# Seven products instead of eight for seven pairs of weight chunks, summed in PSUM; the first w_out chunk cut by column halves; slack for single operations of the plan

## The chip, the core and the metric

The kernel runs on one core of a Trainium2 chip. The metric is the device time of the program in microseconds, the median of its runs; beside it stands one profiled execution with a trace of every instruction on TensorE (PE, its weight loads apart as PEld), VectorE (DVE), ScalarE (ACT), GpSimd (POOL) and SyncE (SP, which issues nearly all transfers here).

## What is computed

A memory attention (4 batches, 8 heads, 576 positions, head size 64, 32 memory slots) feeds two MLPs over 2304 tokens of width 512. In the reference's words, cut:

```python
a = softmax(phi)                                   # over the 32 slots
k_m, v_m = einsum("bhsm,bhsd->bhmd", a, k), einsum("bhsm,bhsd->bhmd", a, v)
x = softmax(q @ k_m^T / 8) @ v_m                   # 2304 x 512
h = x @ w_in;  g = maximum(0.01 * h, h)            # d_ff 2048
y = g @ w_out                                      # 2304 x 512
out = ((y @ w_a) * (y @ w_b)) @ w_out2             # d_ff 1536, all fp32
```

The weights are float64 in the reference and come to the kernel as 64-bit words, which it turns into fp32 itself. Most products run in three passes of the fast fp32r format (high x high, high x low, low x high); the first batch's tokens run in plain fp32 against the first chunks.

## The kernel before

**An order written out by a planner.** The code builds a list of operations (`op`), each with its engines and costs, the tiles it reads and writes, a place in the main sequence (`pos`) for the large products, and a `slack` that moves its due time. `Program.order` then walks through time with these costs and writes one fixed queue per engine; `SLACK`, `LEAD`, `START`, `BIAS`, `LAT`, `OVER`, `SPARE` steer it. Each engine runs its queue strictly in order, so what stands first in a queue holds up what stands behind it. SBUF is 29 "slot" tiles and some larger ones, PSUM 8 banks in rooms: "h" (3 banks), "y" (2), "x" (3); in the second MLP "ab" uses the six banks of "h" and "x", and the output products "o" and "os" share the two banks of "y".

**The start.** For batch b and head group g (0 or 1): phi is loaded, its maximum taken (DVE, `nmx`) and exponentiated (ACT), transposed on PE (`ta`, `tz`) into `en`; `km` multiplies it with the keys and values (tiles `kv`, two per group, and `kvr` for the last 64 positions of both groups), `kvn` normalises, `kvt` transposes, and the result goes into `kd` (keys) and `vm` (values). `vw` multiplies `vm` with a chunk of w_in; `sc` are the scores of one piece of queries (x = 0 or 1; for batch 0 piece 0 has 320 columns, piece 1 has 256), DVE makes the softmax of them through the tile `sm` (transpose, maximum, subtract, exponent on ACT, sum, multiply) and transposes them back to `at`. The first MLP's `h` product needs `at` and `vwf`. A piece of batch 0 and its four column blocks (f) is `h_n_f`; ACT applies the leaky rule into `gf`. `y` then multiplies with w_out: in chunk 0 the four tiles `wout_0` to `wout_3` are 128 rows of w_out by 512 columns, and every `y` needs all four. After loading, a weight tile takes two ACT and four DVE operations (`cv_...`) before PE may read it. `warm` runs 38 transposes of the identity on PE at the start, `idle` puts four more after certain early tiles.

**The second MLP** runs in two halves of the tokens (s = 0, 1), each over 12 chunks c of 128 columns of w_a and w_b. In `ab_unit` the two products y w_a and y w_b over two blocks of 512 tokens are seven block products of 512 columns each, by a Strassen-Winograd scheme: a bank X takes four of them one after the other, and ACT copies X out (`t1`, `u6`, `u67`) between two of them. Chunks are then taken in pairs for the output product with w_out2. For a pair there are two forms. **o_unit**: 8 units (2 token blocks, 4 output blocks) of 6 matmuls of 512 columns. **o_part** (where `by_seven` holds): `w2_sums` and `p_sums` make sums of the weights and of the products, and 14 units of 3 matmuls of 512 columns follow, each in its own PSUM group; the sums of each of the seven products over the pairs are kept in seven SBUF tiles, and combined once, after the last pair (`plus`). In the kernel before, `by_seven` holds for the second half's chunks 0 to 7, four pairs. In the first half a third, narrow block of tokens (l = 2, 256 columns) goes through `left_unit` and `o_unit`. The weights of the first `PRE` = 4 chunks of the second MLP are prepared during the first MLP. At the end SP writes the output, each 128x512 unit of the last block in two transfers of 320 and 192 columns.

## Time and profile before

| | |
|---|---|
| median of 3 runs | 787.19 us (787.18 to 787.81) |
| the profiled execution, its own time | 786.36 us |
| its span in the trace | 784.6 us |
| PE busy | 773.4 us (99%) |
| DVE busy | 607.2 us (77%) |
| ACT busy | 379.1 us (48%) |
| granted clock | 1.00 |

1.76 us of the profiled execution lie outside its span, and the median stands 0.83 us above the profiled execution. A busy time of a stretch is the share in which the engine had at least one instruction in work; matmuls overlap, so what one costs is read from start to start. "idle before" in brackets is how long the engine waited before a row, and for what.

### The profile page before, as it was taken

What the parts mean: (1) busy time and instruction counts of PE and PEld (TensorE: products, weight loads), DVE (VectorE), ACT (ScalarE), POOL (GpSimd) and SP (SyncE); (2) the same over time, 40 slices, a digit from 0 to 9 for tenths busy, and PEclk for the clock granted to TensorE, in tenths of its full rate; (3) what the DMA queues carried; (4) which work ended last, traced back from release to release, by engine and by line L of the source; (5) the groups of instructions that cost most, each with busy time, mean ns of one, the idle gap of its engine ahead of it and who ended that gap; (6) DMA issues with size and microseconds to landing.
All of it is one profiled execution on the core that took longest, in us unless ns stands there. A gap on an engine that the chain in (4) does not pass through costs nothing.

```text
span 784.6 us, 12658 instructions
## 1 busy us (share of the span) xinstructions
PE 773.4 (99%) x4822; PEld 663.4 (85%) x4822; DVE 607.2 (77%) x1149; ACT 379.1 (48%) x817; POOL 0.7 (0%) x6
## 2 busy tenths in 40 slices
PE   7899999999999999999999999999999999999997
PEld 6567898989898988998888888888888888888886
DVE  5888988868888865686745899998995667898865
ACT  5767777747465635453445454445332254223210
POOL 0000000000000000000000000000000000000000
PEclk9999999999999999999999999999999999999999
DMA  9993331573247300035867547475488586978503
GB/s 321 384 323 140 99 90 61 192 264 103 82 174 266 124 1 1 1 115 206 293 247 267 185 160 273 161 239 190 164 322 346 178 275 209 354 250 280 179 19 108
DMA packets 56557, 149.99 MB, mean 191 GB/s; under 512 B 7216, under 2 KB 22576, under 8 KB 56496
## 3 DMA queue, kind: packets, MB, share of 16 engines
q1 hardware_dynamic: 56496, 149.18, 54.5%
q8 instruction: 38, 0.62, 0.3%
q14 instruction: 23, 0.19, 0.1%
HBM read 103.55 MB, written 45.61 MB: 190 GB/s over the span
## 4 chain that ended last, share of the span: by engine, by line
PE 95%; DMA 2%; DVE 1%; SPq 0%; ACT 0%; issue 0%
PE y L871 24%; PE abx L1092 17%; PE o L1186 13%; PE h L821 13%; PE abz L1092 8%; PE os L1301 5%; PE aby L1092 4%; PE b L1146 2%; PE a L1146 2%; PE y L867 2%; PE vw L750 2%; DMA kv<-in_kv_dram 1%; DMA phi<-in_phiT_dram 1%; PE h L803 1%; PE km L603 1%; PE sc L667 0%
## 5 line engine op out<-in xcount | busy, mean ns | idle before, releaser
L871 PE MATMUL y<-g,wout 128*128 128x320 f32 (+2 forms) x1104 | 197.2, 333 | 0.0
L871 PEld LDWEIGHTS y<-g,wout 128*128 128x128 f32 x1104 | 175.6, 188 | 16.7 <-issue 2.1
L1092 PE MATMUL abx<-yb_T,wo 128*128 128x512 f32 x432 | 109.7, 389 | 0.0
L1103 ACT COPY t<-abx 128x512 f32<-128x512 f32 x72 | 42.3, 587 | 122.7 <-PE abx L1092 117.6
L1092 PEld LDWEIGHTS abx<-yb_T,wo 128*128 128x128 f32 x432 | 80.6, 188 | 16.4
L1186 PE MATMUL o<-p,wout 128*128 128x512 f32 x384 | 93.6, 389 | 0.0
L1186 PEld LDWEIGHTS o<-p,wout 128*128 128x128 f32 x384 | 71.9, 188 | 15.2 <-DVE osum L1199 0.4
L774 ACT ACTIVATE g<-h 128x256 fp32r<-128x256 f32 (+1 forms) x120 | 49.7, 414 | 52.9 <-PE h L821 50.8
L821 PE MATMUL h<-ahi,vwh 128*128 128x256 f32 (+1 forms) x240 | 72.7, 303 | 0.0
L821 PE MATMUL h<-ahi,vwl 128*128 128x256 f32 (+1 forms) x240 | 71.0, 296 | 0.0
L821 PE MATMUL h<-alo,vwh 128*128 128x256 f32 (+1 forms) x240 | 71.0, 296 | 0.0
L890 DVE TENSOR_TENSOR acc<-y,acc 128x320 f32<-128x320 f32 (+1 forms) x72 | 40.1, 557 | 36.6 <-PE y L871 35.7
L837 DVE TENSOR_TENSOR g<-t,g 128x256 fp32r<-128x256 f32 (+1 forms) x120 | 53.7, 453 | 15.4 <-ACT t L774 14.4
L821 PEld LDWEIGHTS h<-ahi,vwh 128*128 128x128 f32 x240 | 45.4, 189 | 10.2 <-issue 3.6
L774 ACT ACTIVATE t<-h 128x256 f32<-128x256 f32 (+1 forms) x120 | 49.5, 413 | 0.0
L821 PEld LDWEIGHTS h<-alo,vwh 128*128 128x128 f32 x240 | 45.4, 189 | 0.2
L821 PEld LDWEIGHTS h<-ahi,vwl 128*128 128x128 f32 x240 | 45.5, 190 | 0.0
L1100 DVE TENSOR_TENSOR t<-abz,t 128x512 f32<-128x512 f32 x48 | 33.0, 688 | 13.2 <-PE abz L1092 7.6
L1199 DVE TENSOR_TENSOR oacc<-o,oacc 128x512 f32<-128x512 f32 x40 | 27.6, 690 | 16.7 <-PE o L1186 16.2
L1092 PE MATMUL abx<-yb_B,wo 128*128 128x512 f32 x144 | 36.9, 391 | 0.0
L1092 PE MATMUL aby<-yb_B,wo 128*128 128x512 f32 x144 | 36.7, 390 | 0.0
L407 ACT CAST p<-t 128x512 fp32r<-128x512 f32 x32 | 19.9, 621 | 34.7 <-DVE t L1124 22.7
(289 smaller groups left out, 1276.1 us busy)
## 6 DMA issues: line engine op xcount, KB each, us to landing
k_wo<-wo SPq DMA_DIRECT2D x32, 512.0 KB, 4.4
wo<-k_wo SPq DMA_DIRECT2D x32, 512.0 KB, 4.9
raw_wout<-in_w_out_dram SPq DMA_DIRECT2D x24, 512.0 KB, 5.5
raw_win<-in_w_in_dram SPq DMA_DIRECT2D x16, 512.0 KB, 5.2
...
```

What stands on the lines that cost most here:

```text
L774: nc.scalar.activation(dst, src, AF.Prelu, alpha=0.01)
L821: nc.tensor.matmul(T[o], T[w[u]][:, k, fs], T[a[v]][:, k, cols], start=(k == 0 and i == 0), stop=(k == 1 and i == 2))
L837: lambda T, e: engines[e].tensor_tensor(T[g][:, i, 1, to], T[t], T[g][:, i, 0, to].bitcast(F32), op=ALU.subtract),
L871: nc.tensor.matmul(T[o], w[:, u, es], T[g][:, j, v, at:at + m], start=(f == 0 and p == 0), stop=(f == 3 and p == 2))
L890: "DVE", c_dve(m), lambda T: nc.vector.tensor_tensor(T[acc][:, i, :], T[o], T[acc][:, i, :], op=ALU.add),
L1092: nc.tensor.matmul(T[o], T[w][:, which, u, k * P:(k + 1) * P], T[ys[v]][:, k, :], start=first and k == 0 and x == 0, stop=k == 1 and x == ...
L1100: op("DVE", 0.69, lambda T: nc.vector.tensor_tensor(T[to], T[o], T[x], op=ALU.add), r=[o, x], w=[to], tiles=[o, x, to])
L1103: op("ACT", 0.59, lambda T: nc.scalar.copy(T[t], T[X]), r=[X], w=[t], tiles=[X, t])
L1146: nc.tensor.matmul(T[o], T[w][:, k // 2, u, k % 2 * P:(k % 2 + 1) * P], T[ys[v]][:, k, :], start=(k == 0 and x == 0), stop=(k == 3 and x = ...
L1186: nc.tensor.matmul(T[o], T[w][:, u, es], T[g][:, at, v, :], start=(x == 0 and k == 0), stop=(x == 1 and k == 2))
L1199: "DVE", c_dve(size), lambda T: nc.vector.tensor_tensor(T[acc][:, i, :], T[o], T[acc][:, i, :], op=ALU.add),
L1301: nc.tensor.matmul(T[o], lhs(T, u), T[g][:, v, :], start=k == 0, stop=k == 2)
```

## The change

1. **Seven products for seven pairs.** `SEVENS` lists the chunks for each half: 8 to 11 in the first, 0 to 9 in the second, so two pairs and five pairs.
2. **Summed in PSUM.** The 14 units of a pair stand in another order, and several share a bank: products 1, 6, 7 and 4 are added up in one bank, ACT copies the bank out after 1, 6 and 7 (tile `ok`), and DVE adds what is in the bank to one of four sums in SBUF; products 5 and 3 share another bank, product 2 has its own. There is no combination after the last pair; instead each pair adds the copies to the sums.
3. **w_out's first chunk by column halves.** Its four tiles now hold 256 output columns by 256 rows each, so that `y` for output blocks 0 and 1 reads tiles 0 and 1 only.
4. **The start.** The 256-column piece of batch 0 goes first (`FIRST`); batch 0's `km` is three operations that can start with the transfers that are there; copies into `kd` and `vm` are two operations; 22 transposes in `warm` instead of 38, and `idle` only after two tiles of w_in and after batch 0's `en`.
5. **The plan.** New constants, and `NUDGE`, a table that adds a slack to single operations by their number.
6. **The rest.** `PRE` = 5. The last unit of the output product is two units of 320 and 192 columns.

Counted in the queues: PE has 384 matmuls of 512 columns in `o` before and 234 after (and 6 of 320 and 6 of 192), 168 in `os` before and 294 after; all other products are as many as before; fills are 38 + 48 transposes before and 22 + 16 after. DVE has 1144 rows before and 1201 after, ACT 795 and 838, SP 307 and 321.

```diff
-PRE = 4
+PRE = 5
...
-WARM = 38
-SEVEN = 8
-LEAD = 37
...
+FIRST = (1, 0, *range(2, NPIECE))
+KM_FIRST = (((4,), (0, 1), (2, 3)), ((4,), (0, 1), (2, 3)))
+WARM = 22
+SEVENS = ((8, 9, 10, 11), tuple(range(10)))
+LEAD = 57
...
-        o.slack, o.soon = slack, soon
+        o.slack, o.soon = slack + NUDGE.get(o.seq, 0.0), soon
...
-        "wout": lambda c, k: w_out[c * FC + k * P:c * FC + (k + 1) * P, :],
+        "wout": lambda c, k: w_out[c * FC + k * P:c * FC + (k + 1) * P, :] if c else
+        w_out[2 * (k % 2) * P:2 * (k % 2 + 1) * P, k // 2 * 256:(k // 2 + 1) * 256].rearrange("(j p) f -> p j f", p=P),
...
-        if kind == "win" and c == 0:
+        if kind == "win" and c == 0 and k > 1:
...
-        if b < 2:
+        if b == 0:
             idle(en, lambda t: t[:, 0, :], (en, 0))
...
-                if b == 0:
-                    idle(fk, lambda t, i=i: t[:, i, x * n:x * n + P], (fk, i, x))
...
-        ws = [("wout", c, f) for f in range(4)]
+        ws = [("wout", c, f) for f in range(4)] if c else [("wout", 0, 2 * (e // 2) + i) for i in range(2)]
...
     def by_seven(s, c):
-        return s == 1 and c < SEVEN
+        return c in SEVENS[s]
...
-    O_PARTS = ((1, "A11", "B11"), (6, "S2", "T2"), (7, "S3", "T3"), (5, "S1", "T1"), (2, "A12", "B21"), (4, "A22", "T4"), (3, "S4", "B22"))
+    O_PARTS = ((1, "A11", "B11"), (2, "A12", "B21"), (6, "S2", "T2"), (7, "S3", "T3"), (4, "A22", "T4"), (5, "S1", "T1"), (3, "S4", "B22"))
...
+        bank = {2: "y", 5: "z", 3: "z"}.get(i, "x")
+        o, g = ("os", s, q, x, bank), ("pb", s, q, right)
+        if i in (1, 2, 5):
+            tile_of(o, "y", [NB2])
...
-                nc.tensor.matmul(T[o], lhs(T, u), T[g][:, v, :], start=k == 0, stop=k == 2)
+                nc.tensor.matmul(T[o], lhs(T, u), T[g][:, v, :], start=i in (1, 2, 5) and k == 0, stop=k == 2, skip_group_check=True)
...
+        if i in (1, 6, 7):
+            k = kept_of(i)
+            if x == 0:
+                tile_of(k, "slot", [2, NB2])
+            op("ACT", 0.59, lambda T: nc.scalar.copy(T[k][:, x, :], T[o]), r=[o], w=[(k, x)], tiles=[o, k])
+            return
+        d, m = {2: (2, 1), 4: (4, None), 5: (7, 7), 3: (3, 6)}[i]
...
-            for i in range({NC2 - 2: 4, NC2 - 1: 1}.get(c, 7) if s else 6):
+            for i in range({NC2 - 2: 6, NC2 - 1: 6}.get(c, 8) if s else 7):
...
+                        last = s == 1 and c == NC2 - 1 and l == 1 and e == 3
+                        for cols in [p[:2] for p in places_of(s, l)] if last else [None]:
+                            queue.append(lambda pos, s=s, c=c, l=l, e=e, cols=cols: o_unit(s, c - 1, l, e, pos, cols))
```

**In the queues, at the start.** SP's queue from the phi of batch 1 on, before (`raw_wout` are the tiles of w_out's first chunk; the q behind them are batch 1's queries):

```order
L557 DMA phi_293<-in_phiT_dram 128x1152
L567 DMA kv_0_0_297<-in_kv_dram 128x1024
L567 DMA kv_0_1_306<-in_kv_dram 128x1024
L567 DMA kv_1_0_331<-in_kv_dram 128x1024
L567 DMA kv_1_1_358<-in_kv_dram 128x1024
L570 DMA kvr_385<-in_kv_rest_dram 64x1024
L464 DMA raw_wout_0_397<-in_w_out_dram 128x512
L464 DMA raw_wout_1_414<-in_w_out_dram 128x512
L464 DMA raw_wout_2_427<-in_w_out_dram 128x512
L464 DMA raw_wout_3_475<-in_w_out_dram 128x512
L645 DMA q_0_493<-in_qT_dram 128x1152
```

The same stretch of SP's queue after:

```order
L562 DMA phi_225<-in_phiT_dram 128x1152
L572 DMA kv_0_0_246<-in_kv_dram 128x1024
L575 DMA kvr_265<-in_kv_rest_dram 64x1024
L572 DMA kv_1_1_272<-in_kv_dram 128x1024
L572 DMA kv_0_1_283<-in_kv_dram 128x1024
L572 DMA kv_1_0_300<-in_kv_dram 128x1024
L469 DMA raw_wout_0_315<-in_w_out_dram 128x2x256
L469 DMA raw_wout_1_341<-in_w_out_dram 128x2x256
L660 DMA q_1_349<-in_qT_dram 128x1152
L660 DMA q_0_373<-in_qT_dram 128x1152
```

The small `kvr` moved ahead of three `kv`, so that a `kv` of group 1 is the last of batch 1's inputs; two of the four w_out tiles moved behind the queries of batch 1.

DVE's queue up to the transpose that gives the first `at`, before (`sm_0` is the 320-column piece, `sm_1` the 256-column piece, each with both halves side by side; `er` is batch 1's):

```order
L542 TENSOR_SCALAR er_82<-es_81 128x2
L543 RECIPROCAL er_82<-er_82 128x2
L697 TENSOR_REDUCE mx_8_85<-sm_1_387 128x16
L698 TENSOR_TENSOR sm_1_387<-sm_1_387,mx_8_85 128x512
L702 TENSOR_REDUCE sr_10_84<-sm_0_361 128x20
L703 TENSOR_SCALAR sr_10_84<-sr_10_84 128x20
L704 RECIPROCAL sr_10_84<-sr_10_84 128x20
L707 TENSOR_TENSOR sm_0_361<-sm_0_361,sr_10_84 128x640
L702 TENSOR_REDUCE sr_8_86<-sm_1_387 128x16
L703 TENSOR_SCALAR sr_8_86<-sr_8_86 128x16
L704 RECIPROCAL sr_8_86<-sr_8_86 128x16
L711 STREAM_TRANSPOSE at_0_479<-sm_0_361 128x640
```

The same part of DVE's queue after:

```order
L547 TENSOR_SCALAR er_82<-es_81 128x2
L548 RECIPROCAL er_82<-er_82 128x2
L712 TENSOR_REDUCE mx_10_83<-sm_0_345 128x20
L717 TENSOR_REDUCE sr_8_86<-sm_1_313 128x16
L718 TENSOR_SCALAR sr_8_86<-sr_8_86 128x16
L719 RECIPROCAL sr_8_86<-sr_8_86 128x16
L713 TENSOR_TENSOR sm_0_345<-sm_0_345,mx_10_83 128x640
L722 TENSOR_TENSOR sm_1_313<-sm_1_313,sr_8_86 128x512
L626 TENSOR_SCALAR kvn_0_428<-km_0_380,er_82 128x256
L726 STREAM_TRANSPOSE at_1_430<-sm_1_313 128x512
```

Piece 1 comes first, the other piece's sum and its two companions stand behind the first `at`, and a `kvn` moved from ACT to DVE ahead of it. In both queues the reduction of batch 1's phi (`nmx`) stands earlier: before it precedes the transposes of piece 0's scores, after it stands behind those of piece 1's.

**In the queues, a pair of the second half.** PE's queue at the output product of chunks 8 and 9 before (`o_1_8_0_e`: second half, chunk 8, token block 0, output block e):

```order
L1186 MATMUL o_1_8_0_0_8021<-p_1_8_0_7854,wout2_8_1_7776 128x512 x3
L1186 MATMUL o_1_8_0_0_8021<-p_1_9_0_7989,wout2_9_1_7797 128x512 x3
L1186 MATMUL o_1_8_0_1_8034<-p_1_8_0_7854,wout2_8_1_7776 128x512 x3
L1186 MATMUL o_1_8_0_1_8034<-p_1_9_0_7989,wout2_9_1_7797 128x512 x3
L1092 MATMUL abx_1_10_7894<-yb_1_T4_0_1_6681,wo_1_10_1_7822 128x512
L1092 MATMUL abx_1_10_7894<-yb_1_T4_1_1_6697,wo_1_10_1_7822 128x512
L1092 MATMUL abx_1_10_7894<-yb_1_T4_0_1_6681,wo_1_10_1_7822 128x512 x2
L1092 MATMUL abx_1_10_7894<-yb_1_T4_1_1_6697,wo_1_10_1_7822 128x512
L1092 MATMUL abx_1_10_7894<-yb_1_T4_0_1_6681,wo_1_10_1_7822 128x512
```

PE's queue in the same pair's output product after (`os_1_4_1_x`: second half, pair 4, columns 1 of 2, the bank x):

```order
L1323 MATMUL os_1_4_1_x_8149<-pb_1_4_T2_8051,w2_1_4_0_7878 128x512 x3
L1107 MATMUL aby_1_11_8173<-yb_1_B21_0_1_6661,wo_1_11_0_7956 128x512
L1107 MATMUL aby_1_11_8173<-yb_1_B21_1_1_6672,wo_1_11_0_7956 128x512
L1107 MATMUL aby_1_11_8173<-yb_1_B21_0_1_6661,wo_1_11_0_7956 128x512 x2
L1107 MATMUL aby_1_11_8173<-yb_1_B21_1_1_6672,wo_1_11_0_7956 128x512
L1107 MATMUL aby_1_11_8173<-yb_1_B21_0_1_6661,wo_1_11_0_7956 128x512
L1323 MATMUL os_1_4_1_x_8149<-pb_1_4_T3_8060,w2_1_4_1_7953 128x512 x3
```

Where the pair was 8 units of 6 matmuls, each into a bank of its own, it is now 14 of 3, and here two of them go into one bank with one product of `ab` (6 matmuls) between them, in which time ACT copies the bank out.

**In the queues, the end.** PE's last rows before:

```order
L1186 MATMUL o_10_1_1_8208<-p_11_1_8161,wout_11_1_8028 128x512 x3
L1186 MATMUL o_10_1_2_8217<-p_10_1_8093,wout_10_1_8008 128x512 x3
L1186 MATMUL o_10_1_2_8217<-p_11_1_8161,wout_11_1_8028 128x512 x3
L1186 MATMUL o_10_1_3_8227<-p_10_1_8093,wout_10_1_8008 128x512 x3
L1186 MATMUL o_10_1_3_8227<-p_11_1_8161,wout_11_1_8028 128x512 x3
```

PE's last rows after:

```order
L1204 MATMUL o_10_1_2_8274<-p_11_1_8225,wout_11_1_8016 128x512 x3
L1204 MATMUL o_10_1_3_0_8284<-p_10_1_8138,wout_10_1_8006 128x320 x3
L1204 MATMUL o_10_1_3_0_8284<-p_11_1_8225,wout_11_1_8016 128x320 x3
L1204 MATMUL o_10_1_3_320_8294<-p_10_1_8138,wout_10_1_8006 128x192 x3
L1204 MATMUL o_10_1_3_320_8294<-p_11_1_8225,wout_11_1_8016 128x192 x3
```

The last unit became two, and the one that ends last has 192 columns.

## Rows read from the trace of the kernel before

**Rows 1.** The page: busy us, share, instructions; PE's busy tenths in 40 slices.

```profile
PE 773.4 (99%) x4822; PEld 663.4 (85%) x4822; DVE 607.2 (77%) x1149; ACT 379.1 (48%) x817; POOL 0.7 (0%) x6
...
PE   7899999999999999999999999999999999999997
```

**Rows 2.** Windows: length, busy us of PE, PEld, DVE, ACT, POOL; clock, DMA share, GB/s.

```profile
20.00:30.00 10.00, 9.21 (x131) 5.53 (x130) 7.35 (x15) 6.08 (x16) 0.00 (x0) 1.00 1.03 361
30.00:40.00 10.00, 8.43 (x75) 5.73 (x76) 9.87 (x22) 8.63 (x22) 0.00 (x0) 1.00 1.02 407
```

**Rows 3.** Timeline of PE: start, busy us, merged matmuls of one kind, count.

```profile
97.59 1.93 PE L871 MATMUL y<-g,wout 128*128 128x320 f32 x12
99.36 0.28 PE L821 MATMUL h<-ahi,vwh 128*128 128x256 f32 x1
...
586.67 1.60 PE L1146 MATMUL a<-yl,wo 128*128 128x256 f32 x12
...
595.04 2.88 PE L1186 MATMUL o<-p,wout 128*128 128x512 f32 x12
597.76 1.52 PE L1092 MATMUL abx<-yb_T,wo 128*128 128x512 f32 x6
```

**Rows 4.** Timeline of PE at the start; in brackets idle time before, and releaser.

```profile
19.98 2.35 PE L750 MATMUL vw<-cv_win,vm 64*32 64x256 f32 x32
22.26 1.09 PE L434 MATMUL warm<-ident,vwf 128*128 128x128 f32 x8
...
30.25 0.42 PE L603 MATMUL km<-kvr,en 64*32 64x128 f32 x8 [0.70 <-DMA kvr<-in_kv_rest_dram]
30.60 1.08 PE L603 MATMUL km<-kv,en 128*32 128x128 f32 x32
31.61 0.42 PE L603 MATMUL km<-kvr,en 64*32 64x128 f32 x8
...
33.01 3.50 PE L803 MATMUL h<-at,vwf 128*128 128x320 f32 x12 [0.33 <-DVE at L711]
...
39.46 2.86 PE L803 MATMUL h<-at,vwf 128*128 128x256 f32 x12 [0.78 <-ACT gf L774]
```

**Rows 5.** Timeline of DVE, from batch 1's phi to the first transposed scores.

```profile
22.92 1.35 DVE L531 TENSOR_REDUCE nmx<-phi 128x2 f32<-128x1152 f32 x1 [1.91 <-DMA phi<-in_phiT_dram]
24.31 0.91 DVE L688 STREAM_TRANSPOSE sm<-sc 128x320 f32<-128x320 f32 x2
...
28.97 0.81 DVE L702 TENSOR_REDUCE sr<-sm 128x20 f32<-128x640 f32 x1
29.82 0.17 DVE L703 TENSOR_SCALAR sr<-sr 128x20 f32<-128x20 f32 x1
30.03 0.28 DVE L704 RECIPROCAL sr<-sr 128x20 f32<-128x20 f32 x1
...
32.17 0.79 DVE L711 STREAM_TRANSPOSE at<-sm 128x640 f32<-128x640 f32 x1
```

**Rows 6.** Timeline at the end: DVE's last row, SP's last issues; a transfer's landing.

```profile
780.69 0.69 DVE L1199 TENSOR_TENSOR osum<-o,osum 128x512 f32<-128x512 f32 x1 [0.67 <-PE o L1186]
...
780.05 2.17 SPq L1205 DMA_DIRECT2D out_dram<-osum  x4
...
out_dram<-osum SPq DMA_DIRECT2D x4, 96.0 KB, 1.7
```

**Rows 7.** The tile `warm` from 1.3 to 5.8 us, then 6.3 to 7.9: ns min/median/max.

```profile
L426 PE MATMUL warm<-ident x21: 421/421/473, 1.4 to 5.7; 128*128 128x128 f32 x21
...
L426 PE MATMUL warm<-ident x16: 273/273/290, 6.1 to 7.8; 128*128 128x128 f32 x16
```

**Rows 8.** ACT's copies of the bank X: ns of one; idle us, times.

```profile
L1103 ACT COPY t<-abx x72: 578/587/590, 372.3 to 761.4; 128x512 f32<-128x512 f32 x72
...
  PE abx L1092: 117.6, 62
```

**Rows 9.** DVE alone in a window: length, busy us, clock, DMA share, GB/s.

```profile
431.96:528.24 96.28, 86.14 (x164) 1.00 0.59 202
```

More of the change, by code (lines that the diff above doesn't have):

```diff
@@ L531, in phi_stats @@
             "DVE", c_dve(S * len(gs)), lambda T: nc.vector.tensor_reduce(st[0][:, part], T[phi], axis=AX.X, op=ALU.max, negate=True),
-            r=e, w=nmx, tiles=[phi],
+            r=e, w=nmx, tiles=[phi], slack=SLACK["nmx"] if b else 0.0,
         )
@@ L596, in kv_part, with k_m @@
         tile_of(km, "x", [P])
-        def k_m(T):
-            for t in range(5):
+        def k_m(T, ts, first, last):
+            for t in ts:
                 n = P if t < 4 else 64
-                src = T[kvt[t // 2]][:, t % 2, :] if t < 4 else T[rest][:, g, :]
+                src = T[kvt[t // 2]][:, t % 2, :] if t < 4 else T[rest][:, g, 0:512]
                 for h in range(4):
@@ L604, in k_m @@
                         T[km][h * M:(h + 1) * M, :], T[en][0:n, t, h * M:(h + 1) * M], src[:, h * P:(h + 1) * P],
-                        start=(t == 0), stop=(t == 4),
+                        start=first and t == ts[0], stop=last and t == ts[-1], skip_group_check=True,
                     )
-        op("PE", 1.5, k_m, r=[(en, 0), (en, 1), *kvt, rest], w=[km], tiles=[en, *kvt, rest, km])
+        parts = KM_FIRST[g] if b == 0 else ((0, 1, 2, 3, 4),)
+        for i, ts in enumerate(parts):
+            need = list(dict.fromkeys(kvt[t // 2] if t < 4 else rest for t in ts))
+            op(
+                "PE", 0.29 * len(ts) + 0.05, lambda T, i=i, ts=ts: k_m(T, ts, i == 0, i == len(parts) - 1),
+                r=[(en, 0), *([(en, 1)] if 4 in ts else []), *need], w=[km], tiles=[en, *need, km],
+            )
         def norm(T, e):
@@ L670, in s_sc @@
                         )
-        op("PE", 4 * n / 2.4e3 + TURN, s_sc, r=[*qs, *(("kd", b % 2, g) for g in range(2))], w=scs, tiles=[*qs, *scs])
+        op("PE", 4 * n / 2.4e3 + TURN, s_sc, slack=SLACK["sct", x] if b == 0 else 0.0, r=[*qs, *(("kd", b % 2, g, i) for g in range(2) for i in range(2))], w=scs, tiles=[*qs, *scs])
         NM = n // 32
@@ L717, in sc_both @@
             lambda T, e: engines[e].tensor_tensor(T[alo][:, :, cols], T[at], T[ahi][:, :, cols].bitcast(F32), op=ALU.subtract),
-            r=[at, kh], w=[kl], tiles=[at, ahi, alo], slack=SLACK["sc", min(b, 2), x], ahead=1e12 if whole(0, b) else 60.0,
+            r=[(at, 0), (at, 1), kh], w=[kl], tiles=[at, ahi, alo], slack=SLACK["sc", min(b, 2), x], ahead=1e12 if whole(0, b) else 60.0,
         )
@@ L1314, in o_part @@
         tok = lambda i: (acc(i), x)
-        def plus(d, a):
-            op(
-                two(NB2), 0, lambda T, e: engines[e].tensor_tensor(part(T, d), part(T, d), part(T, a), op=ALU.add),
-                r=[tok(a)], w=[tok(d)], tiles=[acc(a), acc(d)], ahead=1e12, soon=True,
-            )
-        if q == 0:
-            op({"ACT": c_act(NB2), "DVE": c_dve(NB2)}, 0, lambda T, e: copy(e, part(T, i), T[o]), r=[o], w=[tok(i)], tiles=[o, acc(i)])
-            return
-        last = q == SEVEN // 2 - 1
@@ L1326, in o_part @@
-        op("DVE", 0.69, lambda T: nc.vector.tensor_tensor(part(T, i), T[o], part(T, i), op=ALU.add), r=[o], w=[tok(i)], tiles=[o, acc(i)])
-        if not last:
-            return
-        for d in {1: (2, 6), 6: (7, 3), 7: (4,), 5: (3, 7)}.get(i, ()):
-            plus(d, i)
+        kept_of = lambda j: ("ok", s, q, j)
+        if i in (1, 6, 7):
[4 more added lines that the diff above has]
+            return
@@ new lines, in o_part, with into @@
+        d, m = {2: (2, 1), 4: (4, None), 5: (7, 7), 3: (3, 6)}[i]
+        def into(T):
+            return T[acc(d)][:, x, :]
+        if q == 0 and m is None:
+            op({"ACT": c_act(NB2), "DVE": c_dve(NB2)}, 0, lambda T, e: copy(e, into(T), T[o]), r=[o], w=[tok(d)], tiles=[o, acc(d)])
+            return
+        k = kept_of(m) if m else None
+        if q == 0:
+            op("DVE", 0.69, lambda T: nc.vector.tensor_tensor(into(T), T[o], T[k][:, x, :], op=ALU.add), r=[o, (k, x)], w=[tok(d)], tiles=[o, k, acc(d)])
+            return
@@ new lines, in o_part @@
+        op("DVE", 0.69, lambda T: nc.vector.tensor_tensor(into(T), T[o], into(T), op=ALU.add), r=[o], w=[tok(d)], tiles=[o, acc(d)])
+        if m:
+            op(
+                two(NB2), 0, lambda T, e: engines[e].tensor_tensor(into(T), into(T), T[k][:, x, :], op=ALU.add),
+                r=[(k, x)], w=[tok(d)], tiles=[k, acc(d)], ahead=1e12, soon=True,
+            )
+        if 2 * q + 2 == NC2:
+            hh, l = PART[d]
+            for at, w_, to in places_of(s, l):
+                op(
+                    "DMA", c_dma(P * w_ * 4), lambda T, at=at, w_=w_, to=to: nc.sync.dma_start(out[:, 2 * hh + x, to:to + w_], T[acc(d)][:, x, at:at + w_]),
+                    r=[tok(d)], tiles=[acc(d)], ahead=1e12,
+                )
```

122 lines of the change are left out of this document (67 added, 55 removed).

## The prediction

> **What bounds the kernel now.** I read the page first: PE is busy 773.4 us of a span of 784.6, and its tenths are nines in all but the first, second and last of 40 slices [rows 1]. The reader should see that the loss is about 11 us and that nearly all of it lies before 40 us and after 780 us. Next the windows and PE's timeline at the start. From 30 to 40 us PE has 8.43 of 10 us, while DVE has 9.87 and ACT 8.63, the most loaded stretch of both [rows 2]. PE's waits there have three kinds of releaser: a transfer (`kvr`, 0.70 us), DVE (the first `at`, 0.33) and ACT (`gf`, 0.78) [rows 4]. Then the end: PE releases DVE's last addition at 780.69, and 3.9 us pass from there to the span's end at 784.6 with the addition, SP's last issues and a landing [rows 6]. Between 40 and 780 us work taken off PE is time gained one for one, as long as ACT and DVE keep pace; so I looked last at what ACT's copies and DVE have to spare there [rows 8, 9].
>
> The sum is made against the profiled execution, 786.36 us, of which 1.76 lie outside the span; the median of the runs is 0.83 above it. I take both as unchanged and apply the difference to the median, 787.19.
>
> **Seven products.** 512-column matmuls follow each other at (597.76 - 595.04)/12 = 0.227 us [rows 3]. A pair of chunks had 8 x 6 = 48 of them and now has 14 x 3 = 42. Three pairs more take the new form, so 18 go: 18 x 0.227 = **-4.1 us**. That is the difference of the counts too: 384 + 168 = 552 matmuls of 512 columns before, 234 + 294 = 528 after, where 6 of the 24 are the last unit, cut in two. No other work of PE changes after the start.
>
> **The last unit in two.** Six of 320 columns at (99.36 - 97.59)/12 = 0.147, and six of 192. The latter cost 0.085 by proportion to 0.227 and at most 1.60/12 = 0.133 by the row of 256 columns [rows 3]. That is 1.39 to 1.68 us for 6 x 0.227 = 1.36: 0.03 to 0.3, and I take **+0.1**, near the proportion.
>
> **The tail.** DVE's last addition falls from 512 to 192 columns. The two kinds of transposes, 0.79 us for 640 columns and 0.91/2 for 320 [rows 5], give about 1.05 ns a column, so 0.69 becomes 0.35: -0.34. Behind it stood two issues of SP and now one; four took 2.17 us [rows 6], 0.54 each, and as issues can overlap what precedes them I take -0.4 of 0 to -0.54. Together **-0.75** (-0.3 to -0.9). Against it: the last `o` units use the two banks of "y", and now additions of the last seven-product pair stand ahead on DVE. One bank can be late by up to one addition, 0.69 [rows 6], which PE then waits. I take **+0.5** (0 to 0.7), since the queue has such an addition directly ahead.
>
> **The first `h`.** Before, PE was held first by the last transfer of batch 1's inputs, `kvr` at 30.25, then ran `km` of group 1 to 32.03, and `h` began at 33.01 when DVE had `at` [rows 4]. After, as many bytes stand ahead of the last of these inputs, so it should land at 30.25 again, but it is `kv_1_0`. Only group 1's `km` follows, 32.03 - 30.60 = 1.43 us, and one `kvt`, two transposes at (7.8 - 6.1)/15 = 0.113 [rows 7], 0.23: `h` could begin at 30.25 + 1.43 + 0.23 = 31.9. For DVE both queues wait for the same phi, 22.92, and reduce it by 24.27 [rows 5]. Behind that the new queue lacks two transposes (0.91), the other piece's sum and its companions (0.81 + 0.17 + 0.28), and has two operations on 512 in place of 640 columns (about 0.3 less, by the slope above); it gains one `kvn`, about 0.4. `at` would be ready at 32.17 + 0.79 - 2.07 = 30.9, so PE and not DVE sets the start: **-1.1** (-2 if the transfer comes earlier, 0 if phi or `kv` come later, as SP's order past them is new). For this the first scores must be there by 21.1, 2.2 us before 23.29. Leaving out the fills of 22.26 (23.29 - 22.26 = 1.03) and starting the scores after half of `vw` (2.28/2 = 1.1) [rows 4] gives just that; what is late there comes out of DVE's margin of 1.0.
>
> ACT's wait at 39.46, 0.78 us [rows 4], comes as four w_out tiles and `gf` share ACT. With two of the four tiles behind batch 1's queries in SP's queue, half of that conversion leaves the stretch: **-0.6** (-0.8 to 0). The queries come two tiles earlier than that by the queue, so the scores that now stand between `h` products are covered, with about 0.8 us to spare.
>
> **What the new form asks of ACT and DVE.** ACT now has to copy a bank while PE runs one product of 6 matmuls, 6 x 0.227 = 1.36 us. The trace shows such copies at 587 ns, with ACT waiting for PE ahead of 62 of 72 [rows 8]: covered, unless the copy queues behind something of its own length. The queues have 36 such places; each can cost 0 or some tenths. DVE's load is the larger question. From the first addition of chunk 3 to that of chunk 8 of the first half it was busy 86.14 us in 96.28, in 164 instructions of 0.525 us on average [rows 9]. The new queue has 177 there: 93 us, in a stretch that gets no shorter than 95 (no seven-product pair ends in it, only the sums of its weights and `PRE`'s shift move). 98% against 89%. PE's slack there is the buffers' depth. I take **+1.0** for all of this: 0 by the covered copies, 6 if a sixth of a us is lost at each hand-off.
>
> The sum: -4.1 + 0.1 - 0.75 + 0.5 - 1.1 - 0.6 + 1.0 = -4.9, so **782.3 us** (the profiled execution 781.4, its span 779.7). With the bounds of the single terms, which won't fall on one side together, this case runs from 780.2 to 784.5; a start that gives nothing is inside it.
>
> **The rivals.** *The clock at the start.* Of the first 38 transposes the early ones last 0.421 us and those from 6.1 us on 0.273 [rows 7]: PE's pace rose after some 23 of them, back to back. The granted clock reads 1.00 in all windows [rows 2], the 2.4 GHz level, so the slow pace is seen in durations alone. With 22 the chain ends at about the point where the pace rose, and most of the fills behind it are gone. If PE keeps the slow pace until `h`, the `km`, `kvt` and `h` that now set the end are run at it: 0.7 us for the chain of 1.43 + 0.23 ahead of `h` (loads and waits in it don't double), and 2.4 for the first 4.75 us of dense work at half speed, the 4.75 being what the transposes took from 1.35 to 6.1. 782.3 + 3.1 = 785.4. For it: the row at 6.1. Against it: `ta`, `km`, `vw` and 16 fills still keep PE at work with gaps of under 1 us, except ahead of 30.25.
>
> The Trainium skill, "TensorE: Matmul & The Clock Gate", Part 4, says that PE's transposes do not count as busy for the clock gate. The trace disagrees, since the pace rose in a run of nothing but transposes [rows 7]. By the page the shorter `warm` would cost nothing and this rival would fall to the fills' share; by the rows it keeps its chance.
>
> *DVE becomes the bound of the first half* (the slower side). If DVE keeps idling a tenth of that stretch, as the row has it (10.1 of 96.28) [rows 9], because its work comes in the order of PE's banks, 93 + 10 = 103 us are needed where PE needs 95: PE waits 7.9 us for `ab` banks and sums where I put 1.0: 782.3 - 1.0 + 7.9 = 789.2. It decides from waits of about 7.5 us on. For it: 98%. Against it: an idle DVE was waiting for PE, and one that is behind does not idle.
>
> *Some of both*: hand-offs or DVE cost 3 to 5 us in place of 1: 784.3 to 786.3. *The start gives more* (both waits gone and the transfer earlier, no stall at the hand-offs): 779.3 to 780.5. That the change does not do what it says is excluded by the counts of the queues, 528 against 552.
>
> **How the numbers follow.** Forecast 0.58, clock 0.16, some of both 0.09, more 0.08, DVE the bound 0.09. About 0.2%, 1.6 us, is what a measurement can tell from no change: faster below 785.6, slower above 788.8. Faster: 0.58 + 0.08, 0.11 of the clock's 0.16 and 0.05 of the mixed case, 0.82. Within: 0.05 + 0.04 = 0.09. Slower: 0.09. The range leaves out DVE as the bound, a third of the "more" case and the mixed case's upper end, 0.15: 779.8 to 786.0.
>
> **What would show it.** Right: PE's gain between 40 and 780 us near 4; the first `h` near 31.9, with `kv_1_0` as the releaser ahead of it; no wait of 0.78 for `gf`; `os` rows waiting for ACT only by tenths; DVE over 95% in the first half with PE at 9s; a last addition of 0.35 with one issue behind. Wrong: the first 12 matmuls of `h` taking twice their 3.50 us for as many columns (the clock); rows of `ab` or `os` waiting for DVE by whole us between 430 and 530; `h` waiting for `at` (the scores came late); a bank wait over 0.7 before the last units.

## The result and the profile after

The kernel after takes **781.02 us** (median, 780.34 to 781.57) against 787.5 for the kernel before on the same chip: a ratio of 0.9914, interval 0.9897 to 0.9931. On another chip, beside three of the experiments, it took 781.68 against 787.4: 0.9926, interval 0.9913 to 0.9939. It is 5.7 to 6.5 us faster where 4.9 were forecast; 782.3 was predicted, 779.8 to 786.0 the range. The profiled execution took 781.57 with a span of 779.8, 4.8 us less than the span of before.

The page of after: busy us of each engine, PE's busy tenths, and the granted clock of PE in tenths.

```profile
PE 768.4 (99%) x4762; PEld 658.2 (84%) x4762; DVE 632.2 (81%) x1205; ACT 402.3 (52%) x856; POOL 0.7 (0%) x6
...
PE   7899999999999999999999999999999999999998
...
PEclk8999999999999999999999999999999999999999
```

PE is as full as before [rows 1], with 5.0 us less of work. New is the 8 at the front of the clock's row: before it was 9 throughout. The waits of PE from 40 us on, in the whole of after: us in total, times, the longest.

```profile
PE o L1204 <- DVE osum L1217: 0.5, 1, 0.5
```

So the place of the time is found by cutting the span at three starts of PE: the first `h`, the last `y` (at 375.4, 374.2 and 373.3 us in the three columns) and the last matmul of `o` (780.3, 776.5 and 776.3). "After, again" is the same kernel in a second profiled execution (label e12_after, span 779.6).

| stretch of PE | before | after | after, again | predicted change |
|---|---|---|---|---|
| start to first `h` | 33.01 | 32.85 (-0.2) | 31.90 (-1.1) | -1.1 |
| to the last `y` | 342.4 | 341.3 (-1.1) | 341.4 (-1.0) | -0.6 |
| to the last matmul of `o` | 404.8 | 402.3 (-2.5) | 403.1 (-1.8) | -4.1 + 0.1 + 0.5 + 1.0 = -2.5 |
| to the span's end | 4.3 | 3.3 (-1.0) | 3.3 (-1.1) | -0.75 |
| sum | 784.6 | 779.8 (-4.8) | 779.6 (-5.0) | -4.95 |

The same kernel begins `h` a microsecond apart in two executions, and gives the difference back in the second MLP. These two places are what most of the experiments are about. First the start, PE's timeline in after:

```profile
26.59 0.30 PE L592 MATMUL tz<-ident,phi 128*64 128x128 f32 x1 [1.74 <-ACT phi L542]
...
27.80 1.09 PE L589 MATMUL ta<-ident,phi 128*128 128x128 f32 x4 [0.43 <-DVE er L547]
...
29.03 1.90 PE L608 MATMUL km<-kv,en 128*32 128x128 f32 x32
...
31.21 1.08 PE L608 MATMUL km<-kv,en 128*32 128x128 f32 x32
...
32.85 1.46 PE L816 MATMUL h<-at,vwf 128*128 128x256 f32 x6
```

The `km` of group 0 takes 1.90 us where the same 32 matmuls of group 1 take 1.08, as they did in before [rows 4]. The granted clock tells why. Windows of after: length, busy us of PE, PEld, DVE, ACT, POOL; granted clock, DMA share, GB/s.

```profile
10.00:15.00 5.00, 3.87 (x40) 2.62 (x40) 3.19 (x8) 2.29 (x6) 0.00 (x0) 0.53 1.03 406
15.00:20.00 5.00, 4.39 (x61) 3.16 (x53) 2.89 (x7) 2.90 (x8) 0.00 (x0) 0.79 1.07 371
25.00:30.00 5.00, 2.98 (x30) 2.32 (x34) 4.90 (x12) 3.51 (x9) 0.00 (x0) 0.73 1.03 391
```

1.00 is the 2.4 GHz level and 0.5 the 1.2 GHz level; before, each of these windows reads 1.00. The clock fell at about 10 us, and again at 27 us, after PE had waited 1.74 us for the late phi. And phi was late: the reduction `nmx`, which waits for its landing, started at 24.28 where it had been 22.92 [rows 5]; in the second execution of the same kernel it was 23.25. DVE's timeline of after, then DVE's and PE's of after again:

```profile
24.28 1.35 DVE L536 TENSOR_REDUCE nmx<-phi 128x2 f32<-128x1152 f32 x1 [1.08 <-DMA phi<-in_phiT_dram]
```

```profile
23.25 1.35 DVE L536 TENSOR_REDUCE nmx<-phi 128x2 f32<-128x1152 f32 x1 [1.21 <-DMA phi<-in_phiT_dram]
...
27.99 1.89 PE L608 MATMUL km<-kv,en 128*32 128x128 f32 x32
...
30.26 1.08 PE L608 MATMUL km<-kv,en 128*32 128x128 f32 x32
```

### The profile page after: what moved, and what is told of

It reads as the page before. It is cut to its first block, busy times and chain, and to the rows that moved or that the text cites. A ratio compares the mean times of both kernels' runs of the same rounds, so it can differ in the third digit from the quotient of the medians.

```text
span 779.8 us, 12713 instructions
## 1 busy us (share of the span) xinstructions
PE 768.4 (99%) x4762; PEld 658.2 (84%) x4762; DVE 632.2 (81%) x1205; ACT 402.3 (52%) x856; POOL 0.7 (0%) x6
## 4 chain that ended last, share of the span: by engine, by line
PE 95%; DMA 3%; DVE 1%; SPq 0%; issue 0%
PE y L886 24%; PE abx L1107 17%; PE h L834 12%; PE o L1204 9%; PE abz L1107 8%; PE os_x L1323 5%; PE aby L1107 4%; PE os_z L1323 2%; PE b L1161 2%; PE a L1161 2%; PE y L882 2%; PE vw L765 2%; DMA phi<-in_phiT_dram 1%; PE os_y L1323 1%; DMA raw_win<-in_w_in_dram 1%; PE km L608 1%
## 5 line engine op out<-in xcount | busy, mean ns | idle before, releaser
L787 ACT ACTIVATE g<-h 128x320 fp32r<-128x320 f32 (+1 forms) x120 | 49.9, 416 | 68.1 <-PE h L834 63.8
L834 PE MATMUL h<-ahi,vwh 128*128 128x320 f32 (+1 forms) x240 | 72.1, 300 | 0.0
L834 PE MATMUL h<-ahi,vwl 128*128 128x320 f32 (+1 forms) x240 | 71.0, 296 | 0.0
L834 PE MATMUL h<-alo,vwh 128*128 128x320 f32 (+1 forms) x240 | 71.0, 296 | 0.0
L850 DVE TENSOR_TENSOR g<-t,g 128x320 fp32r<-128x320 f32 (+1 forms) x120 | 53.8, 454 | 10.3 <-ACT t L787 9.4
L1204 PE MATMUL o<-p,wout 128*128 128x512 f32 (+2 forms) x246 | 59.8, 385 | 0.5 <-DVE osum L1217 0.5
L1204 PEld LDWEIGHTS o<-p,wout 128*128 128x128 f32 x246 | 45.6, 188 | 10.3 <-DVE osum L1217 1.1
L787 ACT ACTIVATE t<-h 128x320 f32<-128x320 f32 (+1 forms) x120 | 49.9, 416 | 1.5 <-PE h L834 1.2
L1343 ACT COPY ok<-os_x 128x512 f32<-128x512 f32 x42 | 24.6, 587 | 25.6 <-PE os_x L1323 23.3
L1107 PE MATMUL abz<-yb_B,wo 128*128 128x512 f32 x144 | 36.6, 390 | 0.0
```

The lines of the kernel that those rows point to most:

```text
L787: nc.scalar.activation(dst, src, AF.Prelu, alpha=0.01)
L834: nc.tensor.matmul(T[o], T[w[u]][:, k, fs], T[a[v]][:, k, cols], start=(k == 0 and i == 0), stop=(k == 1 and i == 2))
L850: lambda T, e: engines[e].tensor_tensor(T[g][:, i, 1, to], T[t], T[g][:, i, 0, to].bitcast(F32), op=ALU.subtract),
L1107: nc.tensor.matmul(T[o], T[w][:, which, u, k * P:(k + 1) * P], T[ys[v]][:, k, :], start=first and k == 0 and x == 0, stop=k == 1 and x == ...
L1204: nc.tensor.matmul(T[o], T[w][:, u, es], T[g][:, at, v, here], start=(x == 0 and k == 0), stop=(x == 1 and k == 2))
L1343: op("ACT", 0.59, lambda T: nc.scalar.copy(T[k][:, x, :], T[o]), r=[o], w=[(k, x)], tiles=[o, k])
```

## The experiments

### What the three new pairs are worth

`e3_sev4` takes the three new pairs back and leaves all else of the change.

```diff
-SEVENS = ((8, 9, 10, 11), tuple(range(10)))
+SEVENS = ((), tuple(range(8)))
```

> After, with seven products for the four pairs that had them before (chunks 0 to 7 of the second half) and not for the three new ones; they are summed in PSUM as in after, and all else of the change stays. 18 matmuls of 512 columns more (546 against 528) and 57 fewer instructions of DVE. Theory A (the gain is those 18 matmuls and they cost almost nothing elsewhere): 18 x 0.227 = 4.1 us above after, less up to 0.7 for the bank wait of the last pair, which goes: 784.5 to 785.1. Rival F (the three pairs pay back part of it in hand-offs and on a loaded DVE): 1 to 3 us above after, 782 to 784.

Measured: 787.34 us, level with before beside it (ratio 1.0000, interval 0.9992 to 1.0009) and 5.7 to 6.3 above after's two medians, which come from other chips. More than theory A, and the opposite of rival F. In the traces PE's stretch from the last `y` to the last matmul of `o` takes 408.5 us, 6.2 more than the 402.3 of after, and the 18 matmuls are 4.1 of it. PE's waits from 40 us on give the rest:

```profile
PE abx L1107 <- ACT t L1118: 0.7, 1, 0.7
PE o L1204 <- DVE p L794: 0.5, 1, 0.5
PE o L1204 <- DVE osum L1217: 0.4, 1, 0.4
PE os_x L1323 <- ACT osum L411: 0.3, 1, 0.3
```

1.9 us, where after has 0.5; three of the four lie behind 765 us, where chunks 8 to 11 now end in `o` units that follow on each other. In steps between matmuls longer than usual, which hold these waits and what each costs beyond its idle time, PE lost 3.4 us from the last `y` on, against 1.2 in after: 2.2 more, and 4.1 + 2.2 is the 6.2 to within 0.1. So the new pairs bring their matmuls in full and no price for them shows. Whether the waits belong to the form with four pairs, or to a plan whose constants are those of the kernel with seven, no run tells.

The rest of the change, which this kernel keeps, gives nothing by the median. Its trace shows that this nothing is a difference. Cut at the same three starts, it has 32.05, 341.4, 408.5 and 3.3 us: against before it gains 1.0 us ahead of `h`, 1.0 up to the last `y` and 1.1 at the end, and in the second MLP, where both kernels run as many columns, it loses 3.7. Before lost 0.3 us there in long steps, this kernel 3.4. Adding up in PSUM was not tried without the rest, nor were the halves of w_out's first chunk.

### The clock at the start

`e9_bwarm22` is the kernel before with the shorter `warm` alone.

```diff
-        for _ in range(WARM):
+        for _ in range(22):
```

> Before, with 22 transposes in warm in place of 38 and nothing else moved. If fewer transposes alone make the clock fall at 10 us in this place too, the granted clock of 10 to 20 us is 0.5 to 0.8 in place of 1.00. Theory A: that costs little, since DVE waits for phi until 22.9 in any case and the fills before batch 1's km keep the clock up there: within 0.3 us of before. Rival (the clock rival of the prediction): 1 to 3 us slower than before.

Measured: 788.3 us against 787.15: ratio 1.0012, interval 1.0003 to 1.0021, 1.1 us slower (0.2 to 1.7), the lower end of what the rival said. The clock fell here too; from 10 to 15 us, where before has 1.00:

```profile
10.00:15.00 5.00, 4.58 (x43) 3.71 (x45) 4.73 (x14) 3.78 (x9) 0.00 (x0) 0.72 1.02 344
```

Yet `h` began at 32.83 in that profile, no later than before. What it lost there were two waits at 647 and 649 us, which the profile of before lacks:

```profile
PE abx L1092 <- ACT t L1103: 0.7, 1, 0.7
PE os L1301 <- ACT osum L407: 0.7, 1, 0.7
```

Both stand behind one row of ACT, which waited for the landing of weights written back, `k_wo<-wo`. That row in before, then in `e9_bwarm22`:

```profile
643.10 0.62 ACT L407 CAST pb_T<-pT 128x512 fp32r<-128x512 f32 x1 [0.83 <-DMA k_wo<-wo]
```

```profile
646.56 0.62 ACT L407 CAST pb_T<-pT 128x512 fp32r<-128x512 f32 x1 [4.39 <-DMA k_wo<-wo]
```

So in the execution with a trace a transfer that landed late made the loss, and the start did not. That the clock at the start costs the 1.1 us of the median is not shown.

`e1_warm38` gives after the 38 transposes back, `e2_tzfill` puts 14 transposes where PE waited for phi, and `e10_both` does both. No other instruction moves.

```diff
-        for _ in range(WARM):
+        for _ in range(38):
...
         def t_z(T):
+            for _ in range(14 if (b, g) == (1, 0) else 0):
+                nc.tensor.transpose(T[tz], ident[:, 0:64], ident)
             nc.tensor.transpose(T[tz], ph(T)[:, 4 * P:S], ident)
```

> After, with 38 transposes in warm in place of 22 and no other instruction moved. Theory A (the clock): in the kernel after, the granted clock was 0.53 in 10 to 15 us and 0.73 in 25 to 30 us because PE did too little before, and its second fall, not the first, costs time: tz and ta begin at about 8.0 in place of 6.1, the clock stays at 1.00 to 20 us, but the gap from 24.9 to 26.6 us is as it was, the km of batch 1 still run at half pace from 27.8, and h begins at 32.8 as before: time within 0.3 us of after. Rival B (what is lost at the start is set once, by the shorter warm): the clock stays at 1.00 to 40 us, h begins 0.8 to 1.0 us earlier, time 780.1.

> After, with 14 transposes of the identity put ahead of batch 1's tz, into its bank, where PE waited from 24.9 to 26.6 us; nothing else moved. Theory A: the clock does not fall at 27 us, the km of group 0 takes 1.1 us again in place of 1.9, kvn and at follow, and h begins at 32.0 to 32.3 in place of 32.85; time 0.5 to 0.9 us below after, and the runs of it spread less than the 1.2 us of after. Rival B: the fall has another cause than the waiting, km stays at 1.9, the time stays. Rival C: km is faster, but h waits for at, which has been set by the late phi (24.28 in place of 22.92): gain below 0.2.

> After, with both: 38 transposes in warm and 14 ahead of batch 1's tz. Theory A: clock 1.00 from the start to 40 us, h as in the run with the 14 alone, so that the longer warm adds nothing to it (within 0.2 us). Rival B: the two add up, or the 14 alone do nothing and both together give 0.8 us.

Measured: 783.16, 781.71 and 782.43 us (ratios 0.9942, 0.9933 and 0.9940, each with an interval of 0.0012 to 0.0016 either way). None is faster than after; the 38 alone look 1 to 2 us slower. With the 38 the clock was expected at 1.00 up to 20 us, and it fell all the same. `e1_warm38`, then `e2_tzfill` with 22:

```profile
10.00:15.00 5.00, 3.68 (x40) 2.33 (x40) 2.89 (x7) 2.40 (x5) 0.00 (x0) 0.69 1.03 403
```

```profile
10.00:15.00 5.00, 3.50 (x32) 2.34 (x36) 3.54 (x8) 2.28 (x5) 0.00 (x0) 0.50 1.03 402
```

In this window the four kernels with 38 in the new order (two of them below) read 0.61 to 0.73, the eight profiles with 22 read 0.50 to 0.76. So in the new order the first fall is not shown to come from the shorter `warm`. With the 14 it went as expected, and the clock stayed up. A later window of `e2_tzfill`, and then its PE timeline:

```profile
25.00:30.00 5.00, 4.32 (x58) 3.10 (x62) 4.90 (x11) 3.68 (x10) 0.00 (x0) 1.00 1.02 370
```

```profile
28.95 0.64 PE L610 MATMUL km<-kv,en 128*32 128x128 f32 x16
...
31.31 1.08 PE L610 MATMUL km<-kv,en 128*32 128x128 f32 x32 [0.38 <-DMA kv<-in_kv_dram]
...
32.95 1.25 PE L818 MATMUL h<-at,vwf 128*128 128x256 f32 x5
```

`km` runs at full pace and then waits for the last `kv`, which landed at 31.3. `h` starts as late as in after, for another reason. That `kv` came at 30.25 in `e1_warm38`, where `h` began at 31.89, and at 30.59 in `e10_both` (32.23). The other profiles bear out what went ahead of the second fall: where PE had stood still for 1.40 to 1.86 us ahead of `tz` (six of them), the clock of 25 to 30 us was 0.62 to 0.73; where it had stood for 0.54 to 0.56 (`e3_sev4`, and below `e13_dve1` and `e15_outs38`) or had the 14, it was 1.00. Where neither goes well it is worse; PE's timeline of `e14_outs` (below), granted clock 0.64 from 30 to 35 us:

```profile
31.28 1.93 PE L610 MATMUL km<-kv,en 128*32 128x128 f32 x32
...
33.96 0.38 PE L818 MATMUL h<-at,vwf 128*128 128x256 f32 x1
```

So the start of `h` lies between 31.9 and 34.0 us by two things that change from execution to execution: when phi and the last `kv` land, and whether the clock is down as `km` of group 1 runs. The Trainium skill, "TensorE: Matmul & The Clock Gate", Part 1, says that the point at which the clock rises differs from run to run for one kernel; the trace agrees: from 15 to 20 us, in which it rose, the granted clock was 0.79 and 0.90 in two executions of after.

### The place of `kvr` in the queue

`e11_kvr` issues batch 1's `kvr` two places later; only SP's queue changes.

```diff
+            if (b, g, i) == (1, 0, 1):
+                load_rest(T)
...
-        lambda T: nc.sync.dma_start(T[rest][:, :, 0:512], kv_rest[b]), w=[rest]
+        lambda T: None if b == 1 else load_rest(T), w=[rest]
```

> After, with the transfer of batch 1's kvr (64 partitions) issued two places later in SP's queue, ahead of kv_1_0 and not right behind the first kv; no other instruction moved. Theory D (kvr delays phi): in both kernels the transfer rate falls to 210 to 270 GB/s where a kvr is under way, in the kernel after in 22 to 25 us with phi in flight beside it. Then phi lands at about 23.0 in place of 24.28, nmx begins with it, the whole chain to h moves up, km has its inputs as the last kv lands (about 30.3), and h begins between 31.6 and 32.3: time 0.5 to 1.2 us below after. Rival E: phi's landing is set by the bytes ahead of it, 16 transfers in both, and by when SP issued it; it stays at 24.3, and the time stays.

Measured: 782.03 us, no gain (0.9936, interval 0.9924 to 0.9948). The rate of the transfers did move with `kvr`: from 20 to 25 us it is 402 GB/s in place of 318, and from 25 to 30 us 272 in place of 391. GB/s is the last column, first of after (its next window stands above), then of this kernel:

```profile
20.00:25.00 5.00, 4.12 (x64) 1.25 (x64) 3.54 (x8) 1.93 (x8) 0.00 (x0) 1.00 1.04 318
```

```profile
20.00:25.00 5.00, 3.65 (x63) 0.94 (x48) 3.62 (x7) 1.62 (x6) 0.00 (x0) 1.00 1.04 402
25.00:30.00 5.00, 3.96 (x42) 2.91 (x42) 4.90 (x12) 3.82 (x10) 0.00 (x0) 0.66 1.01 272
```

`nmx` began at 23.49; but it did at 23.25 in after again, so that its 0.8 us against after show nothing. And the last `kv` landed at 31.29, with `h` at 32.92. That a `kvr` slows the transfers beside it is supported, though not whether its 64 partitions are the reason; that its place sets `h` is not.

### A wait for an output of the first half

In `e1_warm38` PE reached 639 us earlier than in after and lost that there. ACT's copy `ok` waits for the landing of an output, whose tile it is to write, and the next product waits for the bank. ACT and PE, in `e1_warm38`, then in after, then in after again:

```profile
639.86 0.59 ACT L1343 COPY ok<-os_x 128x512 f32<-128x512 f32 x1 [2.73 <-DMA out_dram<-oacc]
...
640.50 0.96 PE L1323 MATMUL os_x<-pb_T,wout 128*128 128x512 f32 x3 [1.28 <-ACT ok L1343]
```

```profile
639.20 0.59 ACT L1343 COPY ok<-os_x 128x512 f32<-128x512 f32 x1 [1.05 <-DMA out_dram<-oacc]
...
640.09 0.84 PE L1323 MATMUL os_x<-pb_T,wout 128*128 128x512 f32 x3
```

```profile
639.14 0.59 ACT L1343 COPY ok<-os_x 128x512 f32<-128x512 f32 x1 [1.97 <-DMA out_dram<-oacc]
...
639.78 0.97 PE L1323 MATMUL os_x<-pb_T,wout 128*128 128x512 f32 x3 [0.52 <-ACT ok L1343]
```

The kernel after was run once more for its spread:

> The kernel after as it is, beside the other three of this group and on their chip, since its four runs (780.34 to 781.57) were on record alone. Theory G (the wait of ok for an output's landing comes and goes): median 781 to 782, spread 2 to 4 us, as in the two variants with the same order behind the start (781.7 and 782.0). Rival: 781.0 with a spread of 1.2.

Measured: 781.68 us, 781.20 to 782.17; the median is theory G's, the spread of 1.0 us the rival's. Over the seven profiles that keep this order and have DVE's load as it was, the copy begins at 638.8 to 639.9, while `h` began at 31.9 to 33.3. Where PE comes early it waits: an early start of `h` is taken back here, up to 1.3 us of it in idle time and 1.55 from start to start. `e14_outs` issues these outputs first (the edit stands a second time at the outputs of `o_unit`); `e15_outs38` does that with 38 transposes, and `e16_all` with the 14 ahead of `tz` too.

```diff
-                    r=[tok(d)], tiles=[acc(d)], ahead=1e12,
+                    r=[tok(d)], tiles=[acc(d)], ahead=1e12 if s else 2e12,
...
+            if o.ahead == 2e12:
+                o.late = 0.0
```

> After, with the output transfers of the first half's sums issued as soon as the sums are done (a due time of 0 for them in the plan); SP's order from 617 to 640 us changes, and the place of a few products between 625 and 645 us by it. Theory G: in the run with 38 transposes PE waited 1.28 us at 638.8 us for a copy ok of ACT, which waited 2.73 us for the landing of out_dram<-oacc, whose tile it writes; in after ACT waited 1.05 us for the same and PE lost nothing, but by a margin of 0.2 us. This wait then comes and goes from run to run and is part of the spread of 1.2 to 4 us. With the outputs earlier it is gone: no wait of ok for out_dram, the median as after's best runs, 780.3 to 781.0, spread below 2 us. Rival H: the spread is made at the start (transfers landing up to 1 us later); then the median stays at 781 to 782 with the same spread.

> The same, with 38 transposes in warm in place of 22. Theory G and an earlier start: with the 38, h began at 31.9 and 32.2 us in two runs where it began at 32.85 to 32.95 in three with 22; that gain of 0.6 to 1.0 us was lost at 638.8. Here it stays: 0.5 to 1.0 us below the run with the outputs alone, 779.5 to 780.5. Rival H: the start differs by chance, from run to run; both are alike within 0.3.

> After with the first half's outputs issued first, 38 transposes in warm and 14 ahead of batch 1's tz. Theory: the clock is at 1.00 for batch 1's km (it was in the three runs with fills or by chance, and h then began at 32.0 to 33.0; where it was not, at 31.9 to 34.0), and the wait at 638.8 is gone: median 780.0 to 781.0, spread below 1.5. Rival: the landing of the last kv (30.25 to 31.3) is what spreads h, and neither fill changes it: as the run with outputs and 38, 781.0.

Measured: 781.06, 781.02 and 781.54 us (ratios 0.9923, 0.9920 and 0.9928, intervals of 0.0013 to 0.0015 either way). The wait at 639 us is gone in all three profiles. Of the two kernels with 38 transposes, 0.9942 became 0.9920 by the outputs, some 2 us (intervals 0.9930 to 0.9954 and 0.9907 to 0.9934, which overlap by a little; the runs are from two chips): the wait's 1.55 and some more. With `h` at 31.97 and 32.05, spans of 778.6 and 778.7 are the shortest profiled. The 38 added nothing to the outputs alone (781.02 against 781.06), as rival H had it. And by their medians none of the three is told apart from after, and the spread of `e16_all` is 3.3 us, not below 1.5. So `e16_all`, made to be faster than after, is not shown to be.

What spreads the runs is seen beside them: each run lists its mean granted clock. In `e16_all` the two runs at 0.998 took 780.58 and 780.77, those at 0.994 and 0.992 took 782.99 and 783.90. Over all runs of after and its variants, each against the mean of its own kernel, time and clock go together (correlation -0.63; 0.36 us for each 0.001), though the five runs of after again show none by themselves (0.03). The runs of before mostly list 1.000, those of after 0.993 to 0.998. This is a correlation and not an experiment.

### The tail

`e4_tail` leaves the last unit whole.

```diff
-                        last = s == 1 and c == NC2 - 1 and l == 1 and e == 3
+                        last = False
```

> After with the last unit in one piece, as before: 6 matmuls of 512 columns, one addition of 512, two issues behind it. By the prediction's terms 0.65 us slower (0.75 of the tail less 0.1 on PE); by the traces the tail from PE's end was 3.95 before and 3.05 after, and the two smaller units cost 0.2 more on PE: 0.7 slower. Rival: the issues overlap the landing and the transfer of 96 KB sets the end: within 0.3 us.

Measured: 782.28 us against 781.68 beside it, in intervals that overlap. The profiles are sharper, since all of this lies behind the last product of `os`: from the first matmul of `o` after it to the span's end it is 779.8 - 766.59 = 13.2 us in after, the same in after again, and 780.3 - 766.75 = 13.55 here. So the split gives 0.35 to 0.4 us, between the rival's 0.3 and the theory's 0.65. On PE the two units took 0.95 + 0.75 = 1.70 us for 6 x 0.227 = 1.36, 0.34 more, so the tail behind PE is some 0.7 shorter. DVE's last row, in `e4_tail`, then in after:

```profile
776.60 0.69 DVE L1217 TENSOR_TENSOR osum<-o,osum 128x512 f32<-128x512 f32 x1 [0.67 <-PE o L1204]
```

```profile
776.79 0.36 DVE L1217 TENSOR_TENSOR osum<-o,osum 128x192 f32<-128x192 f32 x1 [0.33 <-PE o L1204]
```

### How near DVE is to the bound

`e13_dve1` computes the sums of the weights prepared in the first half twice.

```diff
-    lambda T, e, name=name, x=x, y=y, alu=alu: engines[e].tensor_tensor(val(T, name), val(T, x), val(T, y), op=alu),
+    lambda T, e, name=name, x=x, y=y, alu=alu: [engines[e].tensor_tensor(val(T, name), val(T, x), val(T, y), op=alu) for _ in range(1 if v else 2)],
```

> After with each sum of weights (w_sums) of the chunks prepared in the second MLP's first half computed twice, 28 instructions of 0.42 us more on DVE, 11.7 us, of them some 20 between the first additions of chunk 3 and chunk 8, where DVE was busy 90.9 of 96.4 us in after. This asks how near DVE is to the bound. Theory A (DVE's idle 5.5 us there can nearly all be used): 90.9 + 8.4 = 99.3, so PE waits about 3 us: 784 to 785. Rival B (DVE's idle is forced by the order of PE's banks, so that it is bound already): PE waits the whole 8 us or more: 789 and above. Rival C (tiles in store cover it, as the work is spread over twelve chunks): within 1 us.

Measured: 782.96 us (0.9948, interval 0.9935 to 0.9960), 1.3 above after beside it. Windows of after and then of this kernel (columns as above):

```profile
430.00:526.00 96.00, 96.00 (x506) 82.83 (x505) 90.45 (x177) 49.34 (x91) 0.00 (x0) 1.00 0.64 226
```

```profile
430.00:526.00 96.00, 95.39 (x497) 81.42 (x496) 94.27 (x193) 47.95 (x89) 0.00 (x0) 1.00 0.61 218
```

DVE is at 98% of the stretch and PE still at 99%. PE's waits from 40 us on in `e13_dve1`, the second of which after has too:

```profile
PE o L1204 <- DVE oacc L1217: 0.6, 2, 0.3
PE o L1204 <- DVE osum L1217: 0.5, 1, 0.5
PE os_z L1323 <- DVE oacc L1357: 0.5, 1, 0.5
```

That is 1.1 us more of idle time. From start to start PE's stretch from the last `y` to the last matmul of `o` grew by 2.3 us (404.6 against 402.3; by 1.5 against the 403.1 of after again, which has a wait of its own at 639 us). It lies between theory A (3 us) and C (1 us), by the trace nearer to A; rival B is out. In after DVE still had room for most of the 3.8 us of busy time between these two rows.

## Where the prediction held, and where not

- **Seven products, -4.1.** Held: the counts and the step of 0.227 are as worked out, PE's stretch from the last `y` shortened by 2.5 and 1.8 with the other three terms in it where 2.5 was forecast, and taking the pairs back cost these 4.1 and 2.2 of waits more.
- **The tail, -0.75, and the last unit, +0.1.** The tail held: 0.7, with an addition of 0.36 where 0.35 was worked out. The mis-sized term is the last unit: 0.34 in place of 0.1, since the 192 columns cost 0.112 each, far from the 0.085 by proportion, and the steps from the last matmul of 320 columns to the first of 192, and from that to the next, took 0.22 and 0.19. Together they give 0.35 to 0.4 in place of 0.65.
- **The bank of "y", +0.5.** Right in kind, too small: one wait for `osum`, of 0.55 in idle time, which from start to start cost 0.71 and 0.11 in the next step, 0.82 where the bounds were 0 to 0.7. The term counted idle time alone. PE's timeline of after has it as

```profile
766.59 1.66 PE L1204 MATMUL o<-p,wout 128*128 128x512 f32 x6 [0.55 <-DVE osum L1217]
```

- **The first `h`, -1.1.** By its number right in one execution (31.90) and wrong in the other (32.85). The steps that failed are "both queues wait for the same phi, 22.92" (23.25 and 24.28) and "it should land at 30.25 again" (up to 31.3). Equal bytes ahead of a transfer did not give equal landings. The condition "PE and not DVE sets the start" held. The 31.90 agrees with the 31.9 of the working by luck: group 1's `km` began at 30.26 there, as forecast, but behind the `km` of group 0 at the low clock, 1.89 us, and no transfer released it. With the `kv` as the releaser at 30.25 it came in `e1_warm38`.
- **ACT's `gf`, -0.6.** Too small twice: the wait is gone altogether and not by half, and it had cost more than its 0.78. In before PE began the row at 39.46 1.16 us after the matmul ahead of it and the next 0.32 after that, where their neighbours are 0.22 apart: 1.05 lost, the whole gain of this stretch. That the order of w_out's tiles did it was not tried alone.
- **Hand-offs and DVE, +1.0.** Too high for what it named: from 40 to 625 us PE waits for nothing, and near 630 us two steps are 0.1 longer than usual. The price lies in one hand-off that the term did not name, the `ok` at 639 us behind an output's landing, 0 to 1.3 us of idle time. DVE's load was worked out too high as well: 90.45 of 96.00 us is 94%, not 98%.
- **The clock rival, 0.16.** Out as it was put: PE did not keep the slow pace until `h`, whose first 12 matmuls, of 256 columns, took 2.75 us in after (3.50 for 320 columns in before). The clock is down in parts of 10 to 31 us in both profiles of after, but 38 transposes don't prevent that in the new order (0.69), and the 1.1 us of the shorter `warm` in the old order, where 3.1 were priced, have a late landing as their only traced cause. It reached the `km` just ahead of `h` in two of the variants' profiles, `e14_outs` (`h` at 33.96) and `e4_tail` (33.31), at a cost of 1 to 2 us.
- **DVE as the bound, 0.09.** Refuted as priced: with DVE busy for 94.3 of 96 us the kernel lost 1.3 us by the median, and PE 1.5 to 2.3 by the traces, not 7.9. Most of what DVE idled was spare time.
- **The median.** The measured gain is 0.8 to 1.6 us larger than the forecast, while the profiles differ by 4.8 to 5.0 as forecast. The profiled execution of before was 0.83 below its median; I carried that offset over as unchanged, and after's was 0.5 above its median in one group and 0.3 below in the other. So it is the offset between one profile and a median that was mis-sized. The waits at 647 and 649 us in the variant of before hint at what its other runs lose; that was not settled.
